# Per-chunk gate tiles turned by VectorE, and two decays spread through DRAM, in an mLSTM cell with a feed-forward block

## The chip, the cores and the metric

The kernel runs on one core of one Trainium2 chip. The metric is the device time of one execution, in microseconds (us). A core has a matrix engine (TensorE, PE in the profile; its weight loads have a row of their own, PEld), a vector engine (VectorE, DVE), a scalar engine (ScalarE, ACT), GpSimd (POOL) and a queue processor (SyncE, SP) that here only issues DMA transfers. The engines run side by side and wait for one another on semaphores.

## The reference

An mLSTM cell for 4 batches and 8 heads (32 pairs, called heads below), 768 time steps and a head size of 40, followed by a two-layer block over the 3072 tokens. Cut to what matters:

```python
for t in range(S):                                   # mLSTM, per batch and head
    m_new  = maximum(f[t] + m, i[t])
    f_stab = exp(f[t] + m - m_new)                   # decay of the state
    i_stab = exp(i[t] - m_new)
    C = f_stab * C + i_stab * outer(v[t], k[t]);  n = f_stab * n + i_stab * k[t]
    y[t] = sigmoid(o[t]) * (C @ q[t]) / maximum(abs(n @ q[t]), 1)
x = y as 3072 tokens x 320
h = x @ w_in                                         # 320 x 2048
out = maximum(0.01 * h, h) @ w_out                   # 2048 x 320
```

## The kernel before

The 768 steps are cut into six chunks of 128 tokens, each of two halves of 64 (`SL`). In a chunk the recurrence is written as masked matrix products; the state passes from half to half, multiplied by one decay per head and half. A chunk of one batch (8 heads) is a "step" `s`; a chunk has four.

**Gates.** `gates(c)` (L301) computes running sums and maxima of the gates with the 32 heads on 32 partitions and the 128 times along the row; `gates_exp(c)` (L329) lets ScalarE form the exponentials. The result is the tile `bu`, 32 partitions x 3 x 128: slot 0 is an exponent, slot 1 a weight of the keys, slot 2 the decay from the start of the half to each time, so that its columns 63 and 127 are the decays of the two halves. `gates_exp` also writes `a` and slot 2 to DRAM (`a_dr`, two DMAs on SP's queue), from where ScalarE's queue (`w`) and SP's (`ea`) read them back, spread over partitions.

**Turning.** Later work needs the gates the other way round, with times on the partitions: `gT`, 128 x heads, is the per-partition bias of the exponentials of L513 (ScalarE) and a factor of the keys in L533 (GpSimd). And the two decays are needed on all partitions: `gL`, read by GpSimd where it multiplies the state, `state_next` (L662). `gates_T` (L352) makes both on PE: two transposes of `bu` (L356) and two of a column of slot 2 broadcast to 128 (L361), into one PSUM tile `tg`; VectorE copies them out (L363 to `gT`, L365 to `gL`, which lies in the spare tile `f0`, two halves taken in turn by even and odd chunks).

**The main loop** (L1265) makes a pass for each c from 1 to 6. A pass runs the feed-forward units of chunk c−1 one by one (index i), and in between puts the cell work of chunk c. There are 28 units from c=2 on: units 0 to 13 are the first layer (`fast_firsts`, L981), units 14 to 27 the second (`fast_units`, L879). Both layers use seven products, p1 to p7, in place of eight, each for two halves of the columns or rows (n = 0, 1). In the first layer a product goes into two PSUM banks `ph` (L997), and VectorE adds the banks to `acts` (`add`, two instructions of L1026), or ScalarE copies them out (L1030); the leaky ReLU is ScalarE's L1022. p3(n) accumulates on top of p5(n) in the same two banks, which p5's adds have read before. The order of units is p1, p6, p7, p4, p2, p5, p3 for c=3 and on (p2, p1, p6, p7, p4, p5, p3 in c=2), each with n = 0 and then 1; so units 10 and 11 are p5(0) and p5(1), units 12 and 13 p3(0) and p3(1). In the second layer a product is `po` (L890), and VectorE and ScalarE take turns in combining them; p1 to p7 come in the order p1, p2, p4, p6, p7, p5, p3.

**Where the cell work stands.** `pairs` (L1260, and `first_pairs` for c=2) names the unit behind which each cell unit goes: `u_parts` of two steps at the start of the pass (behind unit 1 in c=2), `u_mix` of these (which has the transposes `pT`, L774, at its start) after unit 3, `u_parts` of the other two after unit 13, then, after unit 17, `u_gates(c+1)` (which calls `gates_T`) and the other two `u_mix`. So the turning stands between the second layer's p2(1) and the `pT` transposes, once per pass in c=2, 3 and 4 for the chunks 3, 4 and 5. For chunks 1 and 2 it is called elsewhere. `gates(c+1)` goes behind unit 0 in c=2 and behind unit 2 later; `gates_exp(c+1)` behind unit 4 in c=2 and unit 3 later. In c=2 VectorE also mixes weights of the second layer behind units 3, 4, 11 and 12 (L229 to L232).

**Orders and waits.** The order on PE, VectorE, ScalarE and GpSimd is the order in which the program is written (`manual_schedule`, L1236); SP's DMAs are ordered by a scheduler. ScalarE issues DMAs too, in the order of its other instructions: keys, values and `w` of later steps are fetched by `feed_slowly` (L1123) between the units. Every DMA of SP and ScalarE signals one of eight semaphores taken in turn, and waits before it is issued for the earlier transfer that had the same one. PSUM is two pools of four banks: `ph` and `po` have the tag "mm", the cell's tiles and `tg` the tag "c". DMAs through the ordered SP queue all show as L96.

Of the kernel before, what the change touches and what calls it, by code (L numbers as in the profile page):

```python
# [9 lines left out]
F32 = mybir.dt.float32  # L10
# [9 lines left out]
def kernel(  # L20
# [26 lines left out]
    nc = tc.nc  # L47
    B, H, S, D = q.shape
    P = 128
    BH = B * H  # L50
    NB = S // P
# [10 lines left out]
    SL = P // 2  # L62
# [18 lines left out]
    wk = ctx.enter_context(tc.tile_pool(name="wk", bufs=2))  # L81
    psf = ctx.enter_context(tc.tile_pool(name="psf", bufs=4, space=PSUM))
    psc = ctx.enter_context(tc.tile_pool(name="psc", bufs=4, space=PSUM))
    dr = ctx.enter_context(tc.tile_pool(name="dr", bufs=1, space=bass.MemoryType.DRAM))
# [17 lines left out]
    sync, by_act = queues = Ordered(nc.sync), Ordered(nc.scalar)  # L102
# [4 lines left out]
    f0 = gp.tile([P, P], F32, name="f0")  # L107
# [6 lines left out]
    def load_fi(c):  # L114
        t = fi[c] = wk.tile([BH, 2, P], F32, name="fi")
        eng = nc.scalar if c < 3 else sync
        eng.dma_start(t[:, 0, :], f_all[:, ts(c, P)])
        eng.dma_start(t[:, 1, :], i_all[:, ts(c, P)])
# [175 lines left out]

    a_dr = dr.tile([NB, 2, 2, BH, SL], F32, name="a_dr")
    x_dr = dr.tile([NS, Dm, P], F32, name="x_dr")
    gT, gL, dCs = {}, {}, {}
    m0s = {}
    bus = {}
# [29 lines left out]
    def gates_exp(c):  # L329
        sync = nc.sync if c == 1 else queues[0]  # L330
        bu, a, na = bus[c]
        if c == 0:
            nc.scalar.activation(bu[:BH, 1, :], bu[:BH, 0, :], AF.Exp, bias=a[:BH, P - 1 :], scale=1.0)
            return
        for u in range(2):
            at = ts(u, SL)
            last = SL * (u + 1) - 1
            nc.scalar.activation(bu[:, 2, at], a[:, at], AF.Exp, bias=na[:] if u else 0.0, scale=1.0)
            nc.scalar.activation(bu[:, 1, at], bu[:, 0, at], AF.Exp, bias=a[:, last : last + 1], scale=1.0)
        if c > 0:  # L340
            sync.dma_start(a_dr[c, 0].rearrange("u n t -> n u t"), a[:].rearrange("n (u t) -> n u t", u=2))
            if c > 1:
                sync.dma_start(a_dr[c, 1].rearrange("u n t -> n u t"), bu[:, 2, :].rearrange("n (u t) -> n u t", u=2))
            if 1 < c < NB - 2:
                load_fi(c + 2)

    def warm(n):
        t = psf.tile([P, P], F32, name="warm", tag="mm")
        for _ in range(n):
            nc.tensor.matmul(t[:], lhsT=ident[:], rhs=ident[:], start=True, stop=True)  # L350
# [728 lines left out]
    def cell_units(c):  # L1079
        if c == 1:  # L1080
            units = [(fn, c * B + n) for n in range(B) for fn in (u_parts, u_plain)]
            units.insert(2 * B - 2, (u_gates, c + 1))
            return units + [(u_x, s) for s in range(B, 2 * B)]
        units = [(fn, c * B + n + m) for n in range(0, B, 2) for fn in (u_parts, u_mix) for m in range(2)]
        if c + 1 < NB:
            units.insert(2 * B - 2, (u_gates, c + 1))
        return units

    masked = set()
# [26 lines left out]
    def feed(s, parts=(0, 1, 2)):  # L1116
        for i in parts:
            if i < 2:
                load(s, i)
            else:  # L1120
                spread(s)
# [114 lines left out]
    with tc.manual_schedule(engines={E.PE, E.DVE, E.Activation, E.Pool}):  # L1236
        ffs = first_chunk()
        load_late(B, 1)
        load_weights(2)
        feed(B)  # L1240
        load_late(B, 2)
        load_weights(3)
        feed(B + 1)
        for i in range(1, 3):
            load_late(B + 1, i)
        for n in range(2):
            load_weights(QN + n)
        for s in (B + 2, B + 3):
            feed(s)
        load_weights(QN + 2)  # L1250
        order["on"] = False


        ffs = ffs[2:]
        fetch = {6: (3, 4), 10: (5, 6), 16: (7,)}
        place = (5, 7, 9, 11, 14, 16, 17, 19, 21, 22, 24, 26, 28)
        late = {}
        masks = {0: (2, 3), 14: (4, 5)}
        first_pairs = (1, 1, 3, 3, 13, 13, 17, 17, 17)
        pairs = (-1, -1, 3, 3, 13, 13, 17, 17, 17)  # L1260
        sums, mixes = sums_of_weights(), mixed_weights()
        N1 = 14
        now = (None for n in range(2, QN + NF // 2) for _ in narrow_weights(n))
        chores, slow = [], []
        for c in range(1, NB + 1):  # L1265
            if c > 1:
                ffs = ff_units(c - 1)
            cells = cell_units(c) if c < NB else []
            n_ff, n_c = len(ffs), len(cells)
            done = fed = 0  # L1270
            waiting, after = [], []

            def visits(i):
                nonlocal done
                at = place if c == 1 else first_pairs if c == 2 else pairs
                while done < min(n_c, sum(p <= i for p in at)):
                    fn, s = cells[done]
                    fn(s)
                    done += 1
                    if fn is u_mix:  # L1280
                        waiting.append(s)
                    if fn is u_plain and s < 2 * B - 1 or fn is u_parts and s == 2 * B - 1:
                        ahead(s + 1)
                    elif fn is u_mix:
                        after.append(s + 2)
                    elif fn is u_plain:
                        prep_mask(s + 2)
                        ahead(s + 2)

            for i in range(n_ff):  # L1290
                if c == 1:
                    run(now, 0 if i < 2 or 4 < i < 7 else 2 if i < 10 else 3 if i < 14 else 4)
                    for n in fetch.get(i, ()):
                        load_weights(QN + n)
                    if i == 3:
                        split_v(B)
                        prep_mask(B)
                        ahead(B)
                    for n in range(3):
                        if i == (7, 9, 11)[n]:  # L1300
                            split_v(B + 1 + n)
                    if i == 0:
                        load_fi(3)
                for s, steps in lazy.items():
                    if s in late and late[s] > 0:
                        late[s] -= 1
                    else:
                        run(steps, 3)
                for n in masks.get(i, ()) if 1 < c < NB else ():
                    if c * B + n < NS:  # L1310
                        prep_mask(c * B + n)
                if i == 0:
                    visits(-1)
                ffs[i]()
                for _ in range(1 if c > 1 and i < N1 else 2 if i > 5 else 0):
                    while fine and next(fine[min(fine)], fine) is fine:
                        del fine[min(fine)]
                if c == 1 and i >= 24:
                    run(sums, 1)
                if c == 2 and i in (3, 4, 11, 12):  # L1320
                    next(mixes)
                if i == n_ff - 1 and c < NB:
                    sums_of_x(c)
                if chores and (c != 2 or i > 8):
                    while chores and next(chores[0], chores) is chores:
                        chores.pop(0)
                if c + 1 < NB:
                    if i == (1, 0, 2)[min(c, 3) - 1]:
                        gates(c + 1)
                    if i == (3, 4, 3)[min(c, 3) - 1]:  # L1330
                        gates_exp(c + 1)
                visits(i)
                if i >= N1 - 1:
                    for s in waiting:
                        gather_x(s)
                    waiting.clear()
                if i < N1 or i >= N1 + 8:
                    for s in after:
                        ahead(s)
                    after.clear()  # L1340
                while fed < done:
                    fn, s = cells[fed]
                    fed += 1
                    if fn in (u_mix, u_plain):
                        load_late(s + NR, 2)
                        if s + NL < NS:
                            if fn is u_mix:
                                slow.append(s + NL)
                            else:
                                feed(s + NL)  # L1350
                if slow:
                    chores.append(feed_slowly(slow))
                    slow = []
# [31 lines left out]
```

## Time and profile before

| | us |
|---|---|
| median of 3 runs | 476.84 (476.38 to 477.55) |
| profiled execution | 476.36 |
| its span | 474.6 |
| PE busy | 459.5 (97% of the span) |
| VectorE busy | 337.1 (71%) |
| ScalarE busy | 202.4 (43%) |
| GpSimd busy | 170.1 (36%) |
| tg transposes on PE, L356 | 13 of 0.227 |
| tg transposes on PE, L361 | 10 of 0.218 |
| copies on VectorE, L363 and L365 | 6 of about 0.225 and 5 of 0.215 |

The span is the time from the first to the last instruction in the profile; the execution's own time has a little around it. A busy time is the sum over the engine's instructions, so that engines overlap. In the rows below, a line of the chain or of a timeline begins with the start and the duration in us; "x64" counts instructions, "[0.74 <-PE pT L774]" says that the engine stood idle for 0.74 us before and that PE's pT ended the wait. "ACTq" and "SPq" are DMA issues.

### The profile page before, as it was taken

Reading aid. Unit: us, or ns where it says so; the run is one execution under the profiler, and the core shown is the slowest. Engines: PE = TensorE matmul, PEld = TensorE weight load, DVE = VectorE, ACT = ScalarE, POOL = GpSimd, SP = SyncE. Lnnn points to the kernel's source line nnn. Section 1 sums busy time; section 2 is a strip of 40 time slices with the busy share of each in tenths; the row PEclk is TensorE's granted clock in tenths of the full one; section 3 lists DMA queues with packets and bytes.
Section 4 is the critical chain, followed back from the end, with each engine's and each line's share of the span. In section 5 each row is a group of like instructions: output and inputs, shape, how many; then the busy total and the mean of one; then the engine's idle time right before and its main releaser. Section 6 shows DMA issues by size and latency. Waiting matters only on the chain.

```text
span 474.6 us, 14137 instructions
## 1 busy us (share of the span) xinstructions
PE 459.5 (97%) x5715; PEld 414.0 (87%) x5715; DVE 337.1 (71%) x595; ACT 202.4 (43%) x491; POOL 170.1 (36%) x205
## 2 busy tenths in 40 slices
PE   7788989999999999999999999999999999999997
PEld 6677868667788899988899988899988999988997
DVE  3888566788989999769689768688847786104631
ACT  3837896575337521356411367311356311153210
POOL 4331575063355154933114833214822004400020
PEclk9999999999999999999999999999999999999999
DMA  9999898868761584875764775744885113100001
GB/s 116 180 200 189 165 220 224 200 112 162 154 163 40 148 170 113 186 139 121 189 122 88 178 158 130 185 103 100 178 155 133 45 30 84 56 1 2 8 8 41
DMA packets 161041, 59.31 MB, mean 125 GB/s; under 512 B 124304, under 2 KB 151760, under 8 KB 160976
## 3 DMA queue, kind: packets, MB, share of 16 engines
q1 hardware_dynamic: 120848, 51.20, 48.5%
q10 hardware_dynamic: 40128, 7.21, 9.2%
q8 instruction: 45, 0.74, 0.7%
q14 instruction: 20, 0.16, 0.1%
HBM read 51.68 MB, written 6.70 MB: 123 GB/s over the span
## 4 chain that ended last, share of the span: by engine, by line
PE 82%; SPq 6%; DVE 4%; DMA 3%; ACT 2%; POOL 1%; issue 1%; DVEq 0%; ACTq 0%; POOLq 0%
PE ph L997 33%; PE po L890 32%; SPq L96 5%; PE po L855 4%; PE pT L774 3%; PE ph L833 3%; PE sd L686 3%; DMA raw<-in_moe_w_in_dram 1%; DMA acts<-in_moe_w_in_dram 1%; PE sd L692 1%; DMA w<-a_dr 1%; DVE w_out L292 1%; DVE qn L703 1%; DVE S L650 1%; DVE w_out L291 1%
## 5 line engine op out<-in xcount | busy, mean ns | idle before, releaser
L890 PE MATMUL po<-w_out,acts 128*128 128x160 f32 x640 | 89.1, 300 | 0.0
L890 PEld LDWEIGHTS po<-w_out,acts 128*128 128x128 f32 x640 | 87.3, 190 | 0.6 <-ACT acts L1022 0.3
L997 PE MATMUL ph<-xT,w_in 64*128 64x256 f32 x720 | 82.7, 378 | 0.0
L997 PEld LDWEIGHTS ph<-xT,w_in 64*128 64x128 f32 x720 | 69.2, 187 | 8.6 <-issue 0.6
L1026 DVE TENSOR_TENSOR acts<-acts,ph 128x512 f32<-128x512 f32 x60 | 38.4, 683 | 39.5 <-PE ph L997 39.3
L890 PE MATMUL po<-raw,acts 128*128 128x160 f32 x480 | 66.4, 300 | 0.0
L890 PEld LDWEIGHTS po<-raw,acts 128*128 128x128 f32 x480 | 65.4, 190 | 0.3
L1030 ACT COPY acts<-ph 128x512 f32<-128x512 f32 x60 | 32.1, 587 | 46.4 <-PE ph L997 46.4
L662 POOL TENSOR_TENSOR S<-S,f 40x336 f32<-40x336 f32 x36 | 32.1, 891 | 54.7 <-PE pT L774 26.6
L1022 ACT ACTIVATE acts<-acts 128x1024 f32<-128x1024 f32 x30 | 31.6, 1055 | 42.6 <-DVE acts L1026 37.4
L505 POOL TENSOR_TENSOR w<-w,i 128x512 f32<-128x512 f32 x20 | 31.0, 1561 | 49.3 <-DMA w<-a_dr 30.2
L513 ACT ACTIVATE w<-w,gT 128x64 f32<-128x64 f32 x160 | 41.6, 338 | 12.1 <-DMA a_dr<-a 3.8
L703 DVE TENSOR_TENSOR qn<-w,sd 64x384 f32<-64x384 f32 (+1 forms) x80 | 33.4, 418 | 10.8 <-PE sd L686 4.5
L833 PE MATMUL ph<-xT,w_in 64*128 64x256 f32 x320 | 37.0, 382 | 2.6 <-DVE w_in L292 1.4
L855 PE MATMUL po<-w_out,acts 128*128 128x320 f32 x128 | 37.1, 439 | 1.3 <-DVE w_out L292 0.8
L833 PEld LDWEIGHTS ph<-xT,w_in 64*128 64x128 f32 x320 | 30.6, 187 | 6.6 <-ACT xT L822 1.3
L997 PE MATMUL ph<-acts,w 64*128 64x256 f32 x320 | 36.3, 379 | 0.0
L788 POOL TENSOR_TENSOR xb<-xb,den 128x320 f32<-128x320 f32 x16 | 11.6, 728 | 68.2 <-DVE xb L785 68.2
L997 PEld LDWEIGHTS ph<-acts,w 64*128 64x128 f32 x320 | 30.6, 187 | 3.6
L855 PEld LDWEIGHTS po<-w_out,acts 128*128 128x128 f32 x128 | 23.4, 190 | 11.1 <-DVE w_out L292 1.7
L928 POOL TENSOR_TENSOR y<-y,raw 128x160 f32<-128x160 f32 x10 | 9.5, 952 | 57.8 <-ACT y L927 56.8
L578 DVE TENSOR_TENSOR qn<-kqT,ea 64x512 f32<-64x512 f32 x32 | 28.5, 890 | 0.8
(177 smaller groups left out, 726.4 us busy)
## 6 DMA issues: line engine op xcount, KB each, us to landing
rb<-in_k_dram SPq DMA_DIRECT2D x64, 80.0 KB
rb<-in_q_dram SPq DMA_DIRECT2D x64, 80.0 KB
rb<-in_o_gate_dram SPq DMA_DIRECT2D x64, 80.0 KB
ea<-a_dr SPq DMA_DIRECT2D x32, 128.0 KB
raw<-in_moe_w_out_dram SPq DMA_DIRECT2D x6, 640.0 KB
w<-a_dr ACTq DMA_DIRECT2D x24, 128.0 KB
xT<-x_dr SPq DMA_DIRECT2D x32, 96.0 KB
x_dr<-x SPq DMA_DIRECT2D x64, 40.0 KB
```

Of the source, the lines that this page charges most:

```text
L505: nc.gpsimd.tensor_tensor(w, w, cm2.unsqueeze(1).to_broadcast([P, H, SL]), op=ALU.add)
L513: yield nc.scalar.activation(w[:, h, :], w[:, h, :], AF.Exp, bias=gT[c][:, 0, bh : bh + 1], scale=1.0)
L578: nc.vector.tensor_tensor(mixed(s)[rows, 1 - r], d["kqT"][rows, 1].rearrange("p (h t) -> p h t", t=SL), d["ea"][rows], op=ALU.mult,)
L662: nc.gpsimd.tensor_tensor(new, old, g, op=ALU.mult)
L703: nc.vector.tensor_tensor(mixed(s)[toks, u, hs], w[toks, hs], bank[1 - u][to[u][hs.start], hs], op=ALU.mult,)
L833: nc.tensor.matmul(ph[r][:, cols], lhsT=w_row(r, slot, j), rhs=xT[DP * r : DP * (r + 1), slot, cols], start=(slot == 0), stop=(slot == KC ...
L855: nc.tensor.matmul(po[n][:], lhsT=acts[:, f, ts(n, P)], rhs=w_out[:, f, :], start=(f == 0), stop=(f == NF - 1),)
L890: nc.tensor.matmul(bank[:], lhsT=left[:, f, :], rhs=right[:, f, :], start=f == 0, stop=f == KH - 1)
L997: nc.tensor.matmul(bank[r][:, e, :], lhsT=left(r)[rows, e], rhs=right(r)[rows], start=first and e == 0 and m == 0, stop=e == 1 and m == le ...
L1022: nc.scalar.activation(to, z, AF.Prelu, alpha=0.01)
L1026: nc.vector.tensor_tensor(to[:, 2 * r : 2 * r + 2], to[:, 2 * r : 2 * r + 2], bank[r], op=ALU.add)
L1030: nc.scalar.copy(to[:, 2 * r : 2 * r + 2], bank[r])
```

## The change

For chunks 3, 4 and 5 `gates_T` is no longer called (it stays for chunks 0, 1 and 2). In its place:

- `gates_exp` writes the two decays of each head to a new DRAM tile `g_dr`, 32 x 2 values, by one more SP DMA behind the two writes of `a_dr`.
- Behind unit 10, `gates_turned` lets VectorE turn slots 0 and 1 of `bu` itself: four transposes, each of 32 partitions x 2 x 32 into 32 other partitions of `gT`, in blocks of 32 x 32.
- Behind unit 12, `spread_decays` reads the 64 values of `g_dr` to all 128 partitions of `f0`'s half by one DMA in ScalarE's queue. `gL` is now a view of it with head outside and half inside, so that the heads lie two values apart.

In VectorE's order the four transposes come behind the second multiply of L578 and ahead of p5(1)'s adds; in ScalarE's order the read comes behind the fourth `w` load and ahead of the ReLU of p3(1). The orders of PE and GpSimd are otherwise unchanged. Below the new helper functions the lines of the changed kernel are 16 higher (L1026 becomes L1042, L997 becomes L1013).

```diff
+    g_dr = dr.tile([NB, BH, 2], F32, name="g_dr")
...
             if c > 1:
                 sync.dma_start(a_dr[c, 1].rearrange("u n t -> n u t"), bu[:, 2, :].rearrange("n (u t) -> n u t", u=2))
+            if c > 2:
+                sync.dma_start(g_dr[c], bu[:, 2, :].rearrange("n (u t) -> n u t", u=2)[:, :, SL - 1])
             if 1 < c < NB - 2:
                 load_fi(c + 2)
+
+    def gates_turned(c):
+
+        bu = bus.pop(c)[0]
+        g = gT[c] = wk.tile([P, 3, BH], F32, name="gT")
+        for j in range(P // BH):
+            nc.vector.transpose(g[ts(j, BH), :2, :], bu[:, :2, ts(j, BH)])
+
+    def spread_decays(c):
+
+        to = f0[:, ts(c % 2, 2 * BH)]
+        nc.scalar.dma_start(to, g_dr[c].rearrange("n u -> (n u)").partition_broadcast(P))
+        gL[c] = to.rearrange("p (n u) -> p u n", u=2)
...
         units = [(fn, c * B + n + m) for n in range(0, B, 2) for fn in (u_parts, u_mix) for m in range(2)]
-        if c + 1 < NB:
-            units.insert(2 * B - 2, (u_gates, c + 1))
         return units
...
-        first_pairs = (1, 1, 3, 3, 13, 13, 17, 17, 17)
-        pairs = (-1, -1, 3, 3, 13, 13, 17, 17, 17)
+        first_pairs = (1, 1, 3, 3, 13, 13, 17, 17)
+        pairs = (-1, -1, 3, 3, 13, 13, 17, 17)
...
                     if i == (3, 4, 3)[min(c, 3) - 1]:
                         gates_exp(c + 1)
+                    if c > 1 and i == 10:
+                        gates_turned(c + 1)
+                    if c > 1 and i == 12:
+                        spread_decays(c + 1)
```

## The prediction

> **What bounds the kernel now.** I read the page's first part, then the busy time by stretches of the five steady chunks, then the chain of waits, then the timelines of VectorE and ScalarE round the edited places. The page's first and fourth parts:
>
> ```profile
> PE 459.5 (97%) x5715; PEld 414.0 (87%) x5715; DVE 337.1 (71%) x595; ACT 202.4 (43%) x491; POOL 170.1 (36%) x205
> PE 82%; SPq 6%; DVE 4%; DMA 3%; ACT 2%; POOL 1%; issue 1%; DVEq 0%; ACTq 0%; POOLq 0%
> ```
>
> TensorE (PE) is busy for 97% and makes up 82% of the chain; the rest of the chain lies in the start and the tail. By stretches (columns: window in us; length; busy us of PE, its weight loads, DVE, ACT, POOL; clock; DMA):
>
> ```profile
> 128.00:164.00 36.00, 36.00 (x482) 31.49 (x480) 33.03 (x53) 18.40 (x43) 15.23 (x14) 1.00 0.48 114
> 200.00:236.00 36.00, 36.00 (x547) 32.10 (x543) 26.56 (x54) 19.31 (x44) 11.43 (x12) 1.00 0.69 151
> 270.00:306.00 36.00, 36.00 (x549) 32.11 (x540) 26.03 (x51) 19.27 (x43) 12.39 (x13) 1.00 0.69 154
> ```
>
> From 128 us on PE has no gap at all, at the full granted clock of 1.00. So a PE instruction taken out there shortens the run by its own time, and work on another engine costs nothing until PE waits for it. VectorE is far closer to that in the first stretch (pass c=2, 33.03 of 36 us busy) than in c=3 and c=4 (26.56 and 26.03). The chain of waits, at the edited place of the three passes and of the last, which has no transposes there:
>
> ```profile
> 166.00 8.89 PE po L890 x64
> 174.89 0.24 PE tg L356 x2
> 175.12 0.12 PE tg L361 x2
> 175.24 2.01 PE pT L774 x64
> ...
> 315.50 0.24 PE tg L356 x2
> 315.74 0.12 PE tg L361 x2
> 315.86 2.02 PE pT L774 x64
> ...
> 376.80 8.89 PE po L890 x64
> 385.69 2.02 PE pT L774 x64
> ```
>
> Neighbours are equal with and without the four transposes (8.89 before, 2.01 to 2.02 behind), so these cost what the chain gives them.
>
> **The change, part by part.**
>
> *PE loses four transposes per chunk, three times.* 175.24 − 174.89 = 0.35 us, 315.86 − 315.50 = 0.36 us; 0.355 us × 3 = **−1.07 us**. All of it is on the path. (Their rows give 0.227 and 0.218 us each, but they are pipelined: the chain counts.) The psc buffer that tg took goes too; no PE instruction waited for it.
>
> *VectorE loses two copies per chunk* (L363 0.225 us, L365 0.215 us). In c=2:
>
> ```profile
> 175.28 0.23 DVE L363 COPY gT<-tg 128x64 f32<-128x64 f32 x1
> 175.42 0.21 DVE L365 COPY f<-tg 128x64 f32<-128x64 f32 x1
> 176.37 0.72 DVE L781 STREAM_TRANSPOSE hb<-pT 128x512 f32<-128x512 f32 x1 [0.74 <-PE pT L774]
> ```
>
> VectorE waits 0.74 us for pT right behind them: nothing gained.
>
> *VectorE gains four 32x64 transposes per chunk*, behind the second multiply of L578 and ahead of p5(1)'s two adds (L1026). None of that size is in the trace. A fixed part and a slope come from L326 (32x1, 0.14 us) and the transpose of L570 (128x512, 0.692 us): 0.14 + 64 × 0.552/511 = 0.21 us, which the 64-element rows repeat (L365 0.215, L703 64x64 0.220). Ends: 0.14 us, and 0.28 us (L314, 32x128). The dearest transpose, L792's with 1.13 us for 512, is kept for a rival. I take 0.21 us, as the 64-element rows are the nearest. How closely do the four follow each other? L365 starts 0.15 us behind L363, before that has ended; L578, which writes rows 64 to 127, ends at 158.66 + 0.69 = 159.35 and L1026, from row 0, starts at 159.38, 0.03 us after the end. The four write at partitions 0, 32, 64 and 96, so I take the second pattern: 4 × (0.21 + 0.03) = **0.96 us** per chunk (ends 0.6, at 0.15 each, and 1.24, at 0.28 + 0.03).
>
> The Trainium skill ("VectorE: DVE Perf Modes", section "Two Vector instructions with no wait between them") holds an instruction whose output starts in another group of 32 partitions than the last one's until all earlier ones have finished. By that rule all four are held, which speaks against the change; the two starts above agree with it, and without it the four would take 0.6 us.
>
> *What that delays.* The timeline of VectorE in c=2:
>
> ```profile
> 158.66 0.69 DVE L578 TENSOR_TENSOR qn<-kqT,ea 64x512 f32<-64x512 f32 x1
> 159.38 1.28 DVE L1026 TENSOR_TENSOR acts<-acts,ph 128x512 f32<-128x512 f32 x2
> 160.58 1.48 DVE L231 TENSOR_TENSOR raw<-w_out 128x1280 f32<-128x1280 f32 x1
> ```
>
> No idle time stands there. PE's p3(1) adds into the banks that p5(1)'s adds read, so its weight load for the second bank waits for them; it went at 161.19 and the adds end at 159.38 + 1.28 = 160.66. Slack 0.52 us. A delay of 0.96 us leaves PE standing for 0.96 − 0.52 = 0.44 us, **+0.45 us**. Behind the adds wait L231, p3's adds and L703; their PE readers stand behind the same 0.45 us, and VectorE is ahead of PE again at 176.37, where it waits, so I add nothing. In c=3 and c=4 VectorE waits for PE ahead of the same adds:
>
> ```profile
> 228.21 0.69 DVE L578 TENSOR_TENSOR qn<-kqT,ea 64x512 f32<-64x512 f32 x1
> 229.48 1.28 DVE L1026 TENSOR_TENSOR acts<-acts,ph 128x512 f32<-128x512 f32 x2 [0.58 <-PE ph L997]
> ```
>
> Idle 0.58 us plus a slack of 231.60 − 230.77 = 0.83 us: 1.41 us, above 0.96 (c=4: 0.59 us and 301.89 − 301.06). **0**.
>
> *SyncE gains one write per chunk* (64 pieces of 4 bytes) behind the two a_dr writes. Each of those holds SP for 0.43 and 0.38 us (c=2, 156.15 and 156.68), so some 0.45 us; it is moved ahead of the two gate loads, the rb loads and all later transfers. What PE needs from this queue last is xT, whose loads end 6.9 to 9.1 us before the first matmul with it: 0. Ends 0 and, if its wait was as long as SP's longest for a ScalarE transfer (3.9 us), still 0, with 3 us left.
>
> *ScalarE gains one read per chunk* (128 × 256 bytes), between the fourth w load and the relu of p3(1). It waits for the write and for the transfer before it on its completion semaphore; in c=2 that is the second ea read, issued about 164.7 us. ScalarE's order in c=2:
>
> ```profile
> 165.22 0.59 ACTq L1129 DMA_DIRECT2D w<-a_dr  x1
> 166.16 1.04 ACT L1022 ACTIVATE acts<-acts 128x1024 f32<-128x1024 f32 x1
> 169.82 0.39 ACTq L1134 DMA_DIRECT2D kn<-in_k_dram  x1
> 170.26 0.29 ACT L912 COPY raw<-po 128x160 f32<-128x160 f32 x1 [3.06 <-DMA rb<-in_k_dram]
> ```
>
> An a_dr write of 156.68 frees its reader at 158.10, 1.4 us on; with up to twice that the read goes by 168 us. Queued behind it are the relu (read by L911 on VectorE at 170.17), kn's load (which waits to 169.82 anyway) and L912, whose bank PE asks for at 177.25. All have over 1 us. In c=3 and c=4 ScalarE is idle there for about 1.5 us. **0**; the end upward is L549's wait for the S loads, 4.8 us, still inside the 6.6 us that PE leaves L912.
>
> *What is nearer or further.* gT is ready some 15 us earlier, gL is first read by POOL at 190.39 us in c=2, 25 us behind the read's issue. gL is now read with a stride of two words by the L662 multiplies (0.89 us each, POOL 36% busy): at nothing, since POOL's sources are read through a broadcast of eight values already. Two po matmuls now wait for VectorE, as they do at no cost in the last pass (160 po in 21.93 us in every pass).
>
> **The sum.** −1.07 + 0.45 = −0.62 us. The profiled execution took 476.36 us, 474.6 of it the span; it would become 475.74. The median of the runs is 476.84, 0.48 above it: **476.2 us**, −0.13%. What a measurement of this kernel can tell from no change is about 0.3%, 1.43 us here.
>
> **The rivals.**
>
> *A. The transposes overlap or are short* (0.15 us apart): delay 0.6 us against 0.52, stall 0.1 us. 476.84 − 1.07 + 0.1 = 475.9 us. For it L363 and L365; against it the 0.03 us gap behind L578.
>
> *B. More than the four transposes goes.* Faster by over 0.3% needs 1.43 us or more: PE would have to lose 0.48 us per chunk where the chain shows 0.355, and no transposes at all show the same neighbours. About 475.2 us; only if the weight loads behind the changed operand shape are held longer than the chain tells.
>
> *C. Slower: the 32x64 transposes are dear.* One mechanism: p3(1) stands for what p5(1)'s adds are late. With d the time of the four, the cost is (d − 0.52) + 2 × (d − 1.41), and it passes the gain by 1.43 us at d = 1.95 us, 0.49 us each. At L792's 1.13 us each (d = 4.6 with gaps) it is 4.1 + 6.4 − 1.1 = +9.4: 486 us; at 0.6 us each (d = 2.5), 2.0 + 2.2 − 1.07 = +3.1: 480 us. For it: one transpose row runs at 2.2 ns per element, and block moves between partition groups have no row here. Against it: L570 and L781 take 0.69 to 0.71 us for 128x512.
>
> *D. Slower: the read holds ScalarE.* If it waited over 7 us (for a transfer that SP's queue keeps back), L912 frees its bank late and PE stands in each of three passes: 1 us more each gives 476.84 − 0.6 + 3 = 479 us. The longest such hold in the trace is 4.8 us.
>
> **How the numbers follow.** Forecast 0.48, A 0.23, B 0.12 (most of it because the base itself spreads from 476.38 to 477.55), C 0.11, D 0.06. Forecast and A lie within 0.3%, with 0.02 of them over either edge: faster 0.14, same 0.69, slower 0.17. The range from 475.0 to 478.2 takes in B's upper part and C up to d = 1.9 us; left out are the rest of C, D and a corner of B, together 0.2.
>
> **What would show it.** In the changed trace: no tg row in passes c=2 to c=4, 8.89 us of po followed at once by pT; four transposes of about 0.21 us with 0.03 us between them behind L578; a PE gap of some 0.45 us ahead of p3(1) in c=2 and none in c=3 and c=4; the f0 read issued by 168 us in c=2, and L912 not late for p4. The prediction is wrong if a transpose takes 0.4 us or more, if PE gaps stand in c=3 and c=4, or if VectorE's order after the mixes stays late to the end of pass c=2.

## The result and the profile after

The changed kernel took 491.27 us (median of 4 runs, 490.23 to 495.69), the kernel before 477.19 us in the same comparison; the ratio is 1.030, with a 95% interval of 1.0267 to 1.0334. It is 14 us slower, where 0.6 us less was forecast. The profiled execution took 491.9 us, with a span of 490.1 us.

From the page of the changed kernel, busy times, the granted clock of TensorE (40 slices, 9 is 0.9 or more) and the chain by engine:

```profile
PE 465.3 (95%) x5703; PEld 418.8 (85%) x5703; DVE 339.6 (69%) x601; ACT 202.4 (41%) x491; POOL 166.0 (34%) x205
PEclk9998999999999969999999999998999999999999
PE 75%; DMA 8%; SPq 6%; DVE 4%; issue 3%; ACT 3%; DVEq 0%
```

The twelve transposes are gone from PE (5715 instructions, now 5703), yet it is "busy" for longer, and in the chain DMA has gone from 3% to 8% and "issue" from 1% to 3%. In three slices the clock is lower, the first of them in the start. The chain shows where (start, duration):

```profile
141.65 2.02 PE pT L790 x64
...
167.94 0.67 issue
...
169.30 5.34 issue
...
175.88 10.95 PE po L906 x64
186.83 2.02 PE pT L790 x64
...
248.02 8.89 PE po L906 x64
256.91 2.02 PE pT L790 x64
...
338.39 0.59 issue
338.98 1.22 DVE acts L960
340.20 0.14 issue
340.33 14.95 PE po L906 x96
```

The transposes pT stand twice in each pass, so that their starts are marks to measure from. Between the first two, in pass c=2, 45.18 us lie where 35.75 lay before (139.49 to 175.24): 9.43 us more. PE stood for 5.34 us, and the 64 po matmuls behind it took 10.95 us in place of 8.89, as the granted clock was 0.50 from 169.8 to 180.0 us. In c=3 the change did what it says: 8.89 us of po are followed at once by pT, and this stretch is 0.36 us shorter (219.87 to 256.91 is 37.04 us, 37.40 before). In c=4 PE waits again, for 2.58 us and here for VectorE; the clock is 0.50 for 3.4 us behind that, so that 96 po matmuls take 14.95 us (13.28 in e9 below), and the pass loses 4.14 us (289.81 to 364.14 is 74.33 us; 70.19 before). Further 2.16 us were lost ahead of all this: the first pT starts at 141.65 us here and at 139.49 before. That is not the change's, of which nothing has run by then: in the twelve kernels below the same mark lies between 139.2 and 141.5 us. In the four traces that have no stretch of lower clock before it (the kernel before, e3, e9, e11) it lies at 139.2 to 139.5 us; in all others, the changed kernel's among them, the clock was 0.50 for 3.4 to 6.8 us somewhere before 75 us, and it lies at 139.6 to 141.7 us. 9.43 + 4.14 − 0.36 + 2.16, and 0.13 in small pieces, are the 15.5 us by which the spans differ.

What stopped PE shows in the stretches (window, length, busy us of PE, PEld, DVE, ACT, POOL, clock, share of the DMA engines' time, GB/s). First the kernel before:

```profile
160.00:165.00 5.00, 5.00 (x112) 4.29 (x109) 5.00 (x7) 3.17 (x7) 0.50 (x1) 1.00 0.66 161
165.00:170.00 5.00, 5.00 (x101) 4.93 (x91) 4.79 (x12) 2.00 (x2) 0.80 (x1) 1.00 0.78 199
```

The changed kernel:

```profile
160.00:162.00 2.00, 2.00 (x22) 1.87 (x20) 1.92 (x5) 1.27 (x6) 0.00 (x0) 1.00 2.96 27
162.00:167.00 5.00, 5.00 (x63) 4.16 (x64) 4.94 (x9) 1.22 (x3) 0.00 (x0) 1.00 0.49 6
167.00:172.00 5.00, 1.52 (x84) 1.06 (x73) 2.62 (x4) 0.00 (x0) 0.00 (x0) 0.78 0.34 23
```

From 160 to 172 us the DMA engines move 6 to 27 GB/s where they moved 161 to 199. The share of 2.96 in the first row counts packets by their start: they began there and lasted far longer than the 2 us. The trace's records of single packets say which: the small writes go out at 160.60 to 160.78 us (80 packets of 4 bytes, 64 of them the decays); the next read on ScalarE's queue, w from a_dr in packets of 2048 bytes, starts at 161.48, and 16 of its packets take from 3.4 to 9.8 us each. SP's own queue, in which the write stands, starts no packet at all from 162 to 168 us. In the kernel before no packet took over 1 us between 150 and 175 us. What ScalarE made of that:

```profile
160.16 0.53 ACTq L1143 DMA_DIRECT2D w<-a_dr  x1
...
174.50 0.48 ACTq L1143 DMA_DIRECT2D w<-a_dr  x1
175.02 0.59 ACT L529 ACTIVATE w<-w,gT 128x64 f32<-128x64 f32 x2 [11.80 <-DMA rb<-in_k_dram]
...
179.63 0.36 ACTq L360 DMA_DIRECT2D f<-g_dr  x1
```

The second w read is issued at 174.50 us (160.67 before), since it waits on its semaphore for an rb transfer that is held up in SP's queue; two exponentials stand behind it, and ScalarE is idle for 11.80 us. The read-back of the decays comes only after all that.

The terms that I had worked out can be seen too. VectorE in c=2:

```profile
160.86 0.69 DVE L594 TENSOR_TENSOR qn<-kqT,ea 64x512 f32<-64x512 f32 x1
161.58 0.98 DVE L355 STREAM_TRANSPOSE gT<-bu 32x64 f32<-32x64 f32 x4
162.59 1.29 DVE L1042 TENSOR_TENSOR acts<-acts,ph 128x512 f32<-128x512 f32 x2
```

and p3 on PE, in the kernel before:

```profile
158.80 5.35 PE L997 MATMUL ph<-xT,raw 64*128 64x256 f32 x48
```

and in the changed kernel:

```profile
160.96 5.82 PE L1013 MATMUL ph<-xT,raw 64*128 64x256 f32 x48
```

Four transposes take 0.98 us, and the same 48 matmuls 0.47 us more.

### The profile page after: what moved, and what is told of

The parts are those of the page before. It is cut to its first block, busy times and chain, and to the rows that moved or that the text cites. A ratio compares the mean times of both kernels' runs of the same rounds, so it can differ in the third digit from the quotient of the medians.

```text
span 490.1 us, 14131 instructions
## 1 busy us (share of the span) xinstructions
PE 465.3 (95%) x5703; PEld 418.8 (85%) x5703; DVE 339.6 (69%) x601; ACT 202.4 (41%) x491; POOL 166.0 (34%) x205
## 4 chain that ended last, share of the span: by engine, by line
PE 75%; DMA 8%; SPq 6%; DVE 4%; issue 3%; ACT 3%; DVEq 0%
PE ph L1013 32%; PE po L906 29%; SPq L96 6%; PE po L871 5%; PE pT L790 3%; PE sd L702 3%; DMA acts<-in_moe_w_in_dram 2%; PE ph L849 2%; DMA rb<-in_o_gate_dram 1%; DMA ea<-a_dr 1%; DMA w_out<-in_moe_w_out_dram 1%; PE sd L708 1%; DMA S<-in_v_dram 1%; DMA rb<-in_q_dram 1%; ACT w_in L283 1%
## 5 line engine op out<-in xcount | busy, mean ns | idle before, releaser
L906 PE MATMUL po<-w_out,acts 128*128 128x160 f32 x640 | 91.1, 304 | 0.0
L906 PEld LDWEIGHTS po<-w_out,acts 128*128 128x128 f32 x640 | 89.4, 194 | 0.7 <-ACT acts L1038 0.3
L1013 PE MATMUL ph<-xT,w_in 64*128 64x256 f32 x720 | 82.7, 378 | 0.0
L1013 PEld LDWEIGHTS ph<-xT,w_in 64*128 64x128 f32 x720 | 69.2, 187 | 8.6 <-issue 0.6
L906 PE MATMUL po<-raw,acts 128*128 128x160 f32 x480 | 68.3, 305 | 2.6 <-DVE acts L960 2.6
L906 PEld LDWEIGHTS po<-raw,acts 128*128 128x128 f32 x480 | 67.1, 194 | 3.1 <-issue 2.8
L1042 DVE TENSOR_TENSOR acts<-acts,ph 128x512 f32<-128x512 f32 x60 | 38.4, 683 | 38.6 <-PE ph L1013 38.5
L849 PE MATMUL ph<-xT,w_in 64*128 64x256 f32 x320 | 38.5, 393 | 3.2 <-ACT xT L838 2.1
L849 PEld LDWEIGHTS ph<-xT,w_in 64*128 64x128 f32 x320 | 31.8, 194 | 7.6 <-ACT xT L838 2.3
L1013 PE MATMUL ph<-acts,w 64*128 64x256 f32 x320 | 36.3, 379 | 0.0
L1013 PEld LDWEIGHTS ph<-acts,w 64*128 64x128 f32 x320 | 30.6, 187 | 3.6
L871 PEld LDWEIGHTS po<-w_out,acts 128*128 128x128 f32 x128 | 23.4, 190 | 10.9 <-DVE w_out L292 1.3
L594 DVE TENSOR_TENSOR qn<-kqT,ea 64x512 f32<-64x512 f32 x32 | 26.8, 839 | 0.8
```

Source lines behind the costliest of these rows:

```text
L849: nc.tensor.matmul(ph[r][:, cols], lhsT=w_row(r, slot, j), rhs=xT[DP * r : DP * (r + 1), slot, cols], start=(slot == 0), stop=(slot == KC ...
L871: nc.tensor.matmul(po[n][:], lhsT=acts[:, f, ts(n, P)], rhs=w_out[:, f, :], start=(f == 0), stop=(f == NF - 1),)
L906: nc.tensor.matmul(bank[:], lhsT=left[:, f, :], rhs=right[:, f, :], start=f == 0, stop=f == KH - 1)
L1013: nc.tensor.matmul(bank[r][:, e, :], lhsT=left(r)[rows, e], rhs=right(r)[rows], start=first and e == 0 and m == 0, stop=e == 1 and m == le ...
L1042: nc.vector.tensor_tensor(to[:, 2 * r : 2 * r + 2], to[:, 2 * r : 2 * r + 2], bank[r], op=ALU.add)
```

## The experiments

Theory W: the write of 64 pieces of 4 bytes holds up all DMA traffic for some 10 us each time, and the rest follows from this. Rivals: R, the read in ScalarE's queue with its waits; D, VectorE's transposes; and the mere presence of one more transfer in SP's queue and in the turn of the semaphores. Holds are told by the data packets of 1 us and more between 150 and 175 us: their first start, their last end, the longest. (Fetches of instructions, in packets of 16 KB, are left out: they take up to 1.7 us in kernels without a hold too.)

**The write alone** (e1_write_only), the kernel before with

```diff
+            if c > 2:
+                sync.dma_start(g_dr[c], bu[:, 2, :].rearrange("n (u t) -> n u t", u=2)[:, :, SL - 1])
```

> The kernel before, with only the write of the 64 decays (64 pieces of 4 bytes into DRAM) added in passes c=2 to c=4; nobody reads them, TensorE and VectorE keep their old turning. Theory W (the write's tiny pieces hold up all DMA traffic for some 10 us each time): like the changed kernel without its gain, 489 to 493 us, with 2048-byte w reads of 3 to 10 us behind the first write. Theory R (the read in ScalarE's queue, its semaphore and its wait do it): 477 us, no change. Theory D (VectorE's transposes do it): 477 us.

Measured: 484.9 us, ratio 1.0156 (1.0123 to 1.0189). Slow packets from 160.2 to 169.2 us, up to 8.5 us. Stretches of this kernel:

```profile
159.00:161.00 2.00, 2.00 (x22) 1.81 (x20) 1.94 (x4) 1.58 (x7) 0.00 (x0) 1.00 3.06 25
161.00:163.00 2.00, 2.00 (x22) 1.80 (x20) 2.00 (x3) 0.90 (x1) 0.00 (x0) 1.00 0.00 0
163.00:165.00 2.00, 2.00 (x25) 1.51 (x23) 2.00 (x3) 0.00 (x0) 0.00 (x0) 1.00 0.55 14
```

In the second row nothing moves at all. So the write by itself makes the hold, and costs more than half of the 14 us, but not all: 7.9 us of it lie in c=2 (43.65 us from pT to pT), none in c=3 and c=4, where slow packets are seen too (up to 6.2 and 3.3 us) but PE does not stop. Theory W's figure was too high, mostly by what e8 below measures.

**All but the write** (e2_no_write):

```diff
-            if c > 2:
-                sync.dma_start(g_dr[c], bu[:, 2, :].rearrange("n (u t) -> n u t", u=2)[:, :, SL - 1])
...
                     if i == 0:
                         load_fi(3)
+                    if i == 20:
+                        nc.sync.dma_start(g_dr[:].rearrange("c n u -> c (n u)"), ident[:NB, : 2 * BH])
```

> The changed kernel without the three writes; the DRAM tile is filled once in the first pass by 6 rows of 256 bytes from the identity matrix, so that the read and all else stay but the decays of chunks 3 to 5 are wrong values. Theory W: 476.2 us (the sum of the prediction: minus 1.07, plus 0.45). Theory R: 488 to 492 us. Theory D: 488 to 492 us.

Measured: 477.29 us, ratio 0.9999 (0.9981 to 1.0017), no data packet over 1 us between 100 and 400 us. R and D fall as causes by themselves: with the read in place and the transposes in place, but no write, nothing is lost that the time can tell. The forecast's −0.13% lies within the interval, and so does no gain. The chain of this kernel:

```profile
140.35 2.02 PE pT L788 x64
...
176.38 2.02 PE pT L788 x64
...
209.43 2.02 PE pT L788 x64
...
246.47 2.02 PE pT L788 x64
```

c=2 takes 36.03 us between its two pT, 0.28 more than before, c=3 37.04 us, 0.36 less. In kernels without a hold that leave the turning of pass c=2 on PE the first figure is 35.66 to 35.95 us, so some 0.1 to 0.4 us are lost in c=2 on balance, where the prediction had +0.1 (0.45 lost, 0.355 gained).

**Another write at the same place** (e5_write_rows), the kernel before with

```diff
+            if c > 2:
+                sync.dma_start(g_dr[c], bu[:, 2, :].rearrange("n (u t) -> n u t", u=2))
```

> The kernel before, with a third write at the place of the decays' write, of all of slot 2 as 64 pieces of 256 bytes (the same as the second gate write that is there already) to a DRAM tile that nobody reads. It has the same extra turn of the DMA semaphores and the same number of pieces as the write of the decays, with 64 times the bytes. Theory W (4-byte pieces): 477 us, within 0.3% of before. If the place in SP's queue, the semaphore turn or the number of pieces does it: 485 us or more.

Measured: 477.76 us, ratio 1.0003 (0.9985 to 1.0021), no hold. 64 pieces at the same place in queue and semaphore turn cost nothing when each has 256 bytes. So it is the small size, or how the pieces lie. Five more kernels besides, each the kernel before with a write that nobody reads, tell these apart.

**4-byte pieces 512 bytes apart** (e4_write_apart, below) **and 64 bytes apart** (e10_apart_64, with 16 in place of P):

```diff
+    g_dr = dr.tile([NB, BH, 2, P], F32, name="g_dr")
...
+            if c > 2:
+                sync.dma_start(g_dr[c, :, :, 0], bu[:, 2, :].rearrange("n (u t) -> n u t", u=2)[:, :, SL - 1])
```

> The kernel before with the write of the 64 decays added (nobody reads them), but each 4-byte piece goes to its own address 512 bytes from the next. Theory W1 (a small piece costs by itself, whatever lies beside it, about 0.15 us of DRAM work, one after the other): as with the pieces side by side, 483 to 487 us. Theory W2 (pieces that fall into the same short stretch of DRAM must follow one another): 477 us, and no packet over 1.5 us in passes c=2 to c=4.

> The kernel before with the write of 64 pieces of 4 bytes, each 64 bytes from the next, nobody reads them. If the stretch that pieces must share to follow one another is 64 bytes or less: 477 us and no packet over 1.5 us in passes c=2 to c=4. If it is larger (128 to 512 bytes): packets of 3 us and more and 479 to 485 us.

Measured: 477.56 us, ratio 1.0002 (0.9981 to 1.0022), and 477.45 us, ratio 0.9995 (0.9975 to 1.0016). No data packet over 1 us in either. Stretches of e4 and of e10, at the time where the others move nothing:

```profile
161.00:166.00 5.00, 5.00 (x103) 4.27 (x102) 5.00 (x7) 2.80 (x8) 0.00 (x0) 1.00 0.59 143
```

```profile
161.00:163.00 2.00, 2.00 (x22) 1.80 (x20) 2.00 (x3) 0.93 (x1) 0.00 (x0) 1.00 0.79 174
```

The same 64 pieces of 4 bytes do no harm that the time or the packets show once they lie 64 bytes apart; e10 differs from e1 in nothing but the addresses in DRAM. W1 falls, W2 holds.

**64 pieces of 64 bytes side by side** (e7_write_64B):

```diff
+    g_dr = dr.tile([NB, BH, 2, 16], F32, name="g_dr")
...
+            if c > 2:
+                sync.dma_start(g_dr[c], bu[:, 2, :].rearrange("n (u t) -> n u t", u=2)[:, :, SL - 16 :])
```

> The kernel before with 64 pieces of 64 bytes, side by side (the last 16 times of each half of slot 2), nobody reads them. If what counts is that a piece is under some size between 64 and 256 bytes: 483 to 487 us. If what counts is that several pieces share a short stretch (64 bytes or less): 477 us.

Measured: 478.08 us, ratio 1.0022 (0.9993 to 1.005), no data packet over 1 us. Side by side shows no hold where each piece fills 64 bytes.

**Half as many** (e6_write_half):

```diff
+            if c > 2:
+                sync.dma_start(g_dr[c, :, 0:1], bu[:, 2, SL - 1 : SL])
```

**and twice as many in two places** (e11_twice):

```diff
+    g_dr = dr.tile([2, NB, BH, 2], F32, name="g_dr")
...
+            if c > 2:
+                for m in range(2):
+                    sync.dma_start(g_dr[m, c], bu[:, 2, :].rearrange("n (u t) -> n u t", u=2)[:, :, SL - 1])
```

> The kernel before with only one of the two decays written, 32 pieces of 4 bytes 8 bytes apart (256 bytes in all are spanned, as before), nobody reads them. If the hold goes with the number of pieces (W1 and W2 alike): half as long, packets of up to 4 to 5 us behind the first write, and 478 to 480 us, since the slack of TensorE and ScalarE takes most. If any such write starts a fixed hold: 485 us, as with 64.

> The kernel before with the write of 64 pieces of 4 bytes side by side made twice in a row, to two places of DRAM, nobody reads them. If the hold goes with the number of pieces: some 18 to 20 us of slow packets behind the first pair in c=2, where one write gives 9 us and half of one 4 us, and the kernel at 500 us or more. If the two places work side by side: about 9 us, and 485 us.

Measured: e6 479.55 us, ratio 1.0042 (1.0025 to 1.006), slow packets from 161.4 to 165.3 us, up to 3.6 us. e11 486.31 us (two executions), ratio 1.0186 (1.013 to 1.0243), slow packets from 159.5 to 168.4 us, up to 8.2 us. Stretches of e6:

```profile
162.00:164.00 2.00, 2.00 (x22) 1.80 (x20) 2.00 (x3) 1.10 (x2) 0.00 (x0) 1.00 0.29 9
164.00:166.00 2.00, 2.00 (x22) 1.60 (x18) 2.00 (x4) 0.00 (x0) 0.00 (x0) 1.00 0.56 96
```

and of e11:

```profile
161.00:164.00 3.00, 3.00 (x30) 2.45 (x26) 3.00 (x4) 0.24 (x1) 0.00 (x0) 1.00 0.38 10
164.00:167.00 3.00, 1.45 (x89) 1.38 (x88) 1.76 (x3) 0.00 (x0) 0.00 (x0) 1.00 0.37 13
```

Half the pieces over the same 256 bytes: 3.9 us of hold where 64 make 9.0. Twice the pieces in two places: 8.9 us, no longer than one write. So the hold goes with how many pieces fall into one short stretch, and the two places work side by side. How long the stretch is remains open. If it is 64 bytes, 16 pieces make 9.0 and 8 make 3.9 us: an estimate of about 0.5 us per piece in a stretch. But stretches of 128 or 256 bytes fit as well: they hold 32 or 64 pieces in e1 and 2 or 4 in e10, a sixteenth in each case, and a sixteenth of 9.0 us, 0.6 us, is below the 1 us by which holds are told. The expectation of e10, 3 us and more for a longer stretch, did not follow from e1's rate. In one table, packets of the trace between 150 and 175 us:

```
kernel      pieces  bytes  apart     slow packets (us)   longest   ratio
e1          64      4      4         160.2 to 169.2      8.5       1.0156
e11         2 x 64  4      4         159.5 to 168.4      8.2       1.0186
e6          32      4      8         161.4 to 165.3      3.6       1.0042
e10         64      4      64        none                          0.9995
e4          64      4      512       none                          1.0002
e7          64      64     64        none                          1.0022
e5          64      256    256       none                          1.0003
```

**The read-back later** (e8_read_late), the changed kernel with its writes:

```diff
-                    if c > 1 and i == 12:
+                    if c > 1 and i == 18:
                         spread_decays(c + 1)
```

> The changed kernel with the read-back moved from behind unit 12 to behind unit 18, so that it holds nothing of ScalarE ahead of the relu of p3(1); the writes stay. The write alone costs 8 us of the 14. If the read in its place costs the other 6 (theory: in c=4 it puts the relu behind a held transfer): 484 to 486 us, and no TensorE stop in c=4. If the other 6 us come from VectorE's part or from the write beside the changed order: 490 to 492 us.

Measured: 486.29 us, ratio 1.0174 (1.0148 to 1.0201). With the writes there, the read at its place costs 5 us more by the medians, and 4.2 us from the first pT to the last (259.53 against 255.30 us). In c=4 of the changed kernel ScalarE comes late to the relu of p3(1), and VectorE's L927 waits for that:

```profile
322.94 0.54 ACTq L360 DMA_DIRECT2D f<-g_dr  x1
323.53 1.06 ACT L1038 ACTIVATE acts<-acts 128x1024 f32<-128x1024 f32 x1 [2.74 <-DMA rb<-in_k_dram]
...
324.62 3.44 DVE L927 TENSOR_TENSOR acts<-acts 128x1024 f32<-128x1024 f32 x2 [2.71 <-ACT acts L1038]
```

where in the kernel before the relu waits 1.53 us, for a read of w, and L911 (the later L927) not at all:

```profile
306.20 1.06 ACT L1022 ACTIVATE acts<-acts 128x1024 f32<-128x1024 f32 x1 [1.53 <-DMA w<-a_dr]
...
310.48 2.35 DVE L911 TENSOR_TENSOR acts<-acts 128x1024 f32<-128x1024 f32 x2
```

From 324.62 us VectorE is busy almost without a break up to L960, which PE then stands for. In e8 the relu is issued at 318.13 us, L927 does not wait, and two short waits of PE for L960 remain, one in c=3:

```profile
264.72 1.21 DVE acts L960
...
335.47 1.21 DVE acts L960
```

so "no stop in c=4" was not quite right: PE stands for 1.31 us at 264.76 and for 0.50 us at 336.31. By passes, from pT to pT, the later read gains 2.1 us in c=2 and 3.75 us in c=4 and loses 1.6 us in c=3. How much of this is the place of the read and how much the other turn of the semaphores in the held traffic is not separated.

**Decays as two pieces** (e3_rows). VectorE turns slot 2 as well; rows 63 and 127 of the turned tile hold the 32 decays side by side:

```diff
-            nc.vector.transpose(g[ts(j, BH), :2, :], bu[:, :2, ts(j, BH)])
+            nc.vector.transpose(g[ts(j, BH), :, :], bu[:, :, ts(j, BH)])
...
+                    if c > 1 and i == 11:
+                        nc.scalar.dma_start(g_dr[c + 1], gT[c + 1][SL - 1 :: SL, 2, :])
+                    if c > 1 and i == 13:
                         spread_decays(c + 1)
```

> The changed kernel, but VectorE turns slot 2 of the gates too, and the two decays go to DRAM as two pieces of 128 bytes (the turned rows of times 63 and 127) by ScalarE's queue behind unit 11, and are read back behind unit 13. Theory W with the number of pieces as its measure: 476.5 us (the sum, and 4 x 0.07 us more VectorE time ahead of p3(1) in c=2). If any write below 512 bytes followed by reads holds up the traffic: 480 us or more. Theory R: 488 to 492 us.

Measured: 477.8 us, ratio 1.0009 (0.9986 to 1.0032), no data packet over 1 us. The 14 us are gone with the kind of write (e3 also puts it into ScalarE's queue and later; e5, e7 and e10 keep its place); a gain over before is not there.

**The same, with the transposes out of p3's way** (e9_rows_later): units 10, 11, 13 become 15, 16, 18.

> The variant with the decays as two pieces of 128 bytes, with the four transposes behind unit 15 (in the second layer, where p3(1) has gone), the write behind unit 16 and the read behind unit 18. Theory: nothing is left of the hold, and TensorE does not wait for p5(1)'s adds in c=2, so all of the 1.07 us comes in: a ratio of 0.9978, and from one pT to the next in the edited passes 0.36 us less than before, in c=2 too (35.4 us in place of 35.75). Rival: VectorE is late elsewhere in c=2 and the pass stays at 35.7 us or more, ratio 1.000.

Measured: 477.93 us, ratio 1.0008 (0.9991 to 1.0026). The rival was right about the time and about VectorE, not about the place: from the first pT to the second the trace has 35.43 us, 0.32 less than before, as the theory had it, but 33.75 to the next where 32.93 lay before. From the chain of this kernel:

```profile
185.11 1.22 DVE acts L958
186.33 0.14 issue
186.47 13.28 PE po L904 x96
```

PE no longer waits for p5(1)'s adds, but VectorE, which has no time to spare in c=2, is late 10 us further on, and the whole pass (139.52 to 208.70, 69.18 us) is 0.50 us longer than before (68.68).

**Only where VectorE has time** (e12_two_chunks), e3 for chunks 4 and 5 alone:

```diff
-                    if c > 1 and i == 10:
+                    if c > 2 and i == 10:
...
+        if c == 2:
+            units.insert(2 * B - 2, (u_gates, c + 1))
```

> The variant with the decays as two pieces of 128 bytes (transposes behind unit 10, write behind 11, read behind 13), but only for chunks 4 and 5, that is in passes c=3 and c=4, where VectorE has idle time; chunk 3 is turned on TensorE as before. Theory: pass c=2 as before (35.7 us from pT to pT and no late VectorE), 0.3 to 0.36 us less in each of c=3 and c=4, together 0.6 to 0.7 us less, a ratio of 0.9986, which the measurement can hardly tell from 1. Rival: something of the transposes or the two DMAs stays on the path in c=3 and c=4 too, ratio 1.000 and no shorter pT to pT.

Measured: 476.98 us against 477.58, ratio 0.9996 (0.9977 to 1.0015): by time no difference that can be told. In the chain both edited passes show the gain:

```profile
236.62 8.89 PE po L904 x64
245.51 2.02 PE pT L788 x64
...
306.57 8.89 PE po L904 x64
315.46 2.02 PE pT L788 x64
```

From pT to pT 37.03 us in both (37.40 and 37.39 before): 0.36 us each, 0.73 together, or 0.15%. This is the best version found, by the trace; no version beat the kernel before by more than the measurement can tell.

## Why the prediction was wrong

The step that failed is "SyncE gains one write per chunk … 0". I priced the write by what it costs the queue that issues it (0.43 and 0.38 us for the a_dr writes) and took these rows, with pieces of 256 bytes, as the nearest for pieces of 4 bytes side by side. They are the nearest, but the two ends that I gave it (0, and SP's longest wait of 3.9 us) bounded only waits of SP. What the pieces do to the traffic of all queues was in no row of the trace, had no end in the sum, and no rival carried it. e1 puts that term at about +7.5 us (1.56%), and e5 shows that the row I used was right for what it was: 64 pieces of 256 bytes, 0.

"ScalarE gains one read per chunk … 0" was right as long as the traffic flows (e2: the read in place, ratio 0.9999) and worth about 5 us with the writes (491.3 against e8's 486.3). Rival D had the victim right, ScalarE held at a DMA issue, and "a transfer that SP's queue keeps back" as what holds it; but it took the trace's longest hold, 4.8 us, as a limit, and the second w read was held until 174.50 us, with 11.80 us of idle time. It was given 0.06 and 479 us. It is only half this case: what kept SP's queue back was the write ahead in it, and the instruction that was held first was a w read, not the read-back. That ScalarE's lateness stops PE is seen in c=4; in c=2 the chain does not put PE's stop down to it (see the last section).

The other steps:

- PE's four transposes: forecast 0.355 us per pass; 0.36 in c=3 of the changed kernel and of e2, 0.36 and 0.37 in e12. In c=4 of e2, e3 and e9 it is only 0.23 to 0.28 (37.11 to 37.16 us for 37.39); kernels that keep the transposes scatter there as much (37.39 to 37.53). Right.
- The copies at nothing: nothing to see against it.
- Four transposes on VectorE 0.96 us: 0.98 us, with 0.233 to 0.238 us each (forecast 0.21) and 0.01 us between them (forecast 0.03): the two misses cancel, by luck. The Trainium skill ("VectorE: DVE Perf Modes", "Two Vector instructions with no wait between them") has them held one behind the other; they start at 161.577, 161.824, 162.072 and 162.323 us, so that none starts before the last has ended, and the trace agrees. Rival A falls with it, and C too: no transpose is near 0.49 us.
- p3(1) in c=2 0.45 us: 0.47 us. In c=3 and c=4 nothing: the 224 matmuls in which it lies take 24.37 us as before.
- "VectorE is ahead of PE again at 176.37 … I add nothing": too kind. In e2, e3 and e9 the whole of c=2 (two intervals, from the first pT to the first pT of the next pass) is 0.40 to 0.50 us longer than the 68.68 us before, where −0.355 + 0.45 = +0.1 was forecast; kernels without a hold that leave the turning of chunk 3 on PE lie between 68.56 and 68.92 us there. This is what the prediction's last sign of being wrong looked for, VectorE late to the end of pass c=2. In the two places tried, VectorE's extra microsecond comes back somewhere in the pass.

So without the write the sum of −0.6 us comes to about −0.2 by e2's marks (246.02 us from the first pT to the last, against 246.20), and e2's time cannot tell either from zero.

## What to carry to other kernels

Price a new DMA not only by its issue and its latency but by how its pieces fall in DRAM: many pieces of 4 bytes, 4 or 8 bytes apart, held nearly all transfers of the core for 4 to 11 us here, whoever issued them, and the same values as two pieces of 128 bytes, or one piece to each 64 bytes, cost nothing that the time could tell. If a transfer of a kind that the trace has no row for shares the engines with everything else, leave the upper end open in the range, and name the traffic of the others as a rival. Work moved off the bound engine onto one that has no idle time in that stretch comes back as a wait; the three passes here had to be looked at one by one.

## What the runs showed of the hardware

- The hold by pieces that lie close together in DRAM (4 bytes apart 9 us for 64 pieces, 8 bytes apart 3.9 us for 32, 64 bytes apart none seen) was not expected. It stops packets of other queues that go to other addresses: on ScalarE's queue reads of 2048 bytes took up to 9.8 us, 80-byte packets in c=3 up to 4.8 us. Why these must wait, and the length of the stretch that pieces must share, stay open. The Trainium skill ("DMA: Bandwidth & Descriptors", "Specifications") says that below 512 bytes a transfer is done as read-modify-write. That alone does not give what is seen: by it e4, e5, e7 and e10, all of pieces under 512 bytes, should suffer too, and they show no hold; sharing has to come in.
- PE's stop of 5.34 us in c=2 is called "issue", a wait for nothing that the profile shows. Instructions too come by DMA, in packets of 16 KB (45 of them on queue q8), and were held up as well; that q8 carries PE's is inferred, from 45 packets to 11430 matmuls and weight loads, where VectorE, ScalarE and GpSimd have some 1300 instructions together. The queue's row in the kernel before, from 147 to 166 us:

```profile
q8 instruction: 1, 0.02, 0.3%
```

and in the changed kernel, which has no such row from 149 to 172 us and this one from 172 to 174.6:

```profile
q8 instruction: 1, 0.02, 2.2%
```

  The packets' records put this fetch at 161.0 us before, at 161.6 in e4 and at 172.3 in the changed kernel. PE goes on 1.3 to 1.6 us after the late fetch has ended, in the changed kernel (173.2, PE at 174.6), in e1 (170.8, 172.2), e6 (167.0, 168.4), e8 (171.2, 172.6) and e11 (168.8, 170.4). And in all five, whose stops last from 0.9 to 5.3 us, the stop ends at the same matmul, with 2240 before it, and in the changed kernel it ends ahead of the waits of VectorE (175.64 us) and ScalarE (175.02 us), so that it was not for them. That the late fetch is what PE stood for is read from these times and this place; no run held up the fetch by itself.
- From 0.5 us into that stop on the granted clock was 0.50 for 10.2 us (169.8 to 180.0 us), which made 8.89 us of po into 10.95. With the stops of 5.0 and 5.1 us in e1 and e8 it was 0.50 for 6.8 us, behind the 2.58 us in c=4 for 3.4 us, and at stops of 1.3 us and less (e6, e8, e9) it stayed at 1.00. So a stop of 2.58 us and more on PE cost more than its own length here.
